# Attention into a mixer MLP: the first batch's loads cut at head three, and three batches' k pooled on GpSimd instead of TensorE

## The chip, the core and the metric

The kernel runs on one core of a Trainium2 chip. The core has five engines that run at the same time and meet only through semaphores: TensorE (PE) for matrix products, VectorE (DVE) and ScalarE (ACT) for element-wise work, GpSimd (POOL) for element-wise work and for issuing the loads that cast float32 to bf16, and SyncE (SP), which here only issues DMAs: the outputs and the transposing copies. All data moves over 16 DMA engines that the queues share. The metric is the time of one execution in microseconds of the device; smaller is better.

## What is computed

There are 8 batches, 8 heads, 576 rows and 64 columns per head. Keys and values are averaged over groups of 8 rows, so attention runs against 72 pooled rows; the result goes through a mixer (a token MLP over the rows and a channel MLP over the 512 columns), each with a residual.

```python
k_p = k.reshape(B, H, 72, 8, D).mean(axis=3)
v_p = v.reshape(B, H, 72, 8, D).mean(axis=3)
attn = softmax(scale * q @ k_p.T)              # 576 x 72 per head
x = (attn @ v_p) as (B, 576, 512)
u = x + (relu(x.T @ w_tok1) @ w_tok2).T        # 576 -> 256 -> 576
out = u + relu(u @ w_ch1) @ w_ch2              # 512 -> 1536 -> 512
```

## The kernel before

**Tiling.** The 576 rows of a batch are 512 "main" rows (four tiles of 128, row 4p+j in partition p of tile j) and 64 "tail" rows. The tails of two batches share one 128-row tile: the groups are [0,7], [1,2], [3,4], [5,6], the first of a pair in the lower half (slot 0), the second in the upper (slot 1). For groups [3,4] and [5,6] one `TailUnit` does the tail attention of both batches at once, and so needs the pooled keys of both.

**Pooled keys.** `pool_k(b)` (L259) is 32 matmuls of the raw main rows of k against a pooling matrix (L271) and 8 of the tail rows (L275), into two PSUM tiles; then four casts, two on ACT and two on DVE (L284, L285), put them block-diagonally into `kbd[b % 3]`. **Pooled values.** Batches 0 and 1 do the same by matmul (`pool_v`). From batch 2 on, v is loaded as 72 partitions of 8 rows (`vs`, L133 to 136), and GpSimd adds the 8 rows up, `sum_v` (L296): three adds for every two heads, four times, into `vpx[b % 3]`.

**The streams.** Each batch's main work, `c_stream(b)`, is the channel MLP: 12 pieces of four 512-column matmuls (L776), then 12 more (L791), three for each of four output chunks; the third of a chunk adds the residual on DVE (L801) and issues the chunk's output DMA on SP (L829). Every piece has the weight 864. A side stream, the attention of later batches, is woven between these pieces by `weave` (L29): a side item is taken when the share of side weight done is not above the share of main weight done. Main weight counts from `delay` (the second argument, 1728, that is two pieces) to `lead` (the third, 1728) before the end. An item of weight 0 is taken as soon as the item ahead of it is finished in this count. While c_stream(b) runs, the side stream holds `value_stream(b+1)` (start the transposing loads of batch b+2's q, `load_gated` for batch b+3's inputs, attention times values, the token MLP, `do_u`, and `pool_k` of a coming batch) and `score_stream(b+2)`: scores `do_S` (matmuls L330, then maximum and subtraction on DVE, L333 and L335), exponentials `do_E` on ACT (L343), transposes of the probabilities `do_PT` by DMA on SP (L350), for the two units a and c of 256 rows, then the tail unit t (L431, L437, L439, L446, L452).

**Order.** Inside `with tc.manual_schedule(engines=...)` (L854) each engine runs its instructions in exactly the order in which the Python code emits them, SP's DMAs included. Ahead of it, the set-up is ordered by the framework. An engine that waits holds up all that is behind it.

**Gates of the loads.** `load_gated(b)` (L750) first copies one element of a transposed-probability tile on GpSimd, so that the loads of batch b are not issued before; the loads and then the sums for v follow in GpSimd's order. At L739 it is called with b+2 for the batch b whose values are due.

**Batch 0** has a stream of its own (`first_stream`, L604): pool k, transpose q on PE in two halves of four heads, scores, pooled v, and so on.

Of the kernel before, what the change touches and what calls it, by code (L numbers as in the profile page):

```python
# [48 lines left out]
def kernel(  # L49
# [58 lines left out]
    half = [slice(0, TAIL), slice(TAIL, P)]  # L108
    main_t, tail_t = {}, {}
# [9 lines left out]
    def load(b, which=(0, 1, 2)):  # L119
# [9 lines left out]
        for i in which:  # L129
            src = (k, q, v)[i]  # L130
            if i == 2 and b > 1:
# [26 lines left out]
    load_main0(k, main_t[0][0], 0, H)  # L158
    load_tail0(k, tail_t[0][0])

# [7 lines left out]
    nc.gpsimd.memset(pool_m, 1.0 / POOL)  # L168
# [6 lines left out]
    nc.gpsimd.memset(diag, 1.0 / POOL)  # L175
# [5 lines left out]
    for s in range(2):  # L181
        nc.vector.memset(pool_t[s], 0.0)
        nc.vector.tensor_copy(out=pool_t[s][half[s], SPM:SP],
                              in_=diag[half[s], s * (SP - SPM):(s + 1) * (SP - SPM)])
    ident = singles.tile([P, P], BF16)
    make_identity(nc, ident)

    load_main0(q, main_t[0][1], 0, HP)
    load_main0(q, main_t[0][1], HP, H)
# [6 lines left out]
    NB = 3  # L196
    kbd = [singles.tile([P, H, 2, SP], BF16, name=f"kbd{i}") for i in range(NB)]
    vpx = [singles.tile([SP, H, D + 1], BF16, name=f"vpx{i}") for i in range(NB)]
    for i in range(NB):
        eng = nc.vector if i == 0 else nc.any  # L200
        eng.memset(kbd[i], 0.0)
        eng.memset(vpx[i][:, :, D], float(POOL))
# [4 lines left out]
    for g in range(2):  # L207
        x_tail[g] = singles.tile([P, DM], BF16, name=f"xt{g}")
        nc.any.memset(x_tail[g][half[1]], 0.0)
    for t in tail_t[1]:  # L210
        nc.any.memset(t[half[1]], 0.0)

    def clear_probs():
        for t in prob_m:
            nc.any.memset(t.rearrange("p e h n -> p (e h) n")[:, :, SP:P], 0.0)
        for t in prob_t:
            nc.any.memset(t, 0.0)
# [10 lines left out]
    def load_w_tok():  # L228
        for s in range(2):
            nc.any.memset(w1t[s][half[1 - s]], 0.0)  # L230
            nc.any.memset(w2t[s][:, :, half[1 - s]], 0.0)
# [3 lines left out]
        nc.gpsimd.dma_start(out=w1t[1][half[1], :], in_=moe_w_tok1[MAIN:S, :])  # L235
# [26 lines left out]
    def pool_k_sum(b):  # L262
        g, s = group_of[b], slot_of[b]
        km, kt = main_t[b][0], tail_t[b][0]
        kp_ps = [ps.tile([P, HP, SP], FP32, name="pa") for _ in range(2)]
        if b == 0:
            keep_running(kp_ps[0].rearrange("p r n -> p (r n)"), 22)
        for pr in range(HP):
            for j in range(NJ):
                for hl in range(2):  # L270
                    nc.tensor.matmul(out=kp_ps[hl][hl * D:(hl + 1) * D, pr, 0:SPM], lhsT=km[:, 2 * pr + hl, j, :],  # L271
                                     rhs=pool_m[:, 0:SPM], start=(j == 0), stop=(j == NJ - 1))
        for pr in range(HP):
            for hl in range(2):
                nc.tensor.matmul(out=kp_ps[hl][hl * D:(hl + 1) * D, pr, SPM:SP], lhsT=kt[:, 2 * pr + hl, :],  # L275
# [3 lines left out]
    def pool_k_copy(b, kp_ps):  # L279
        heads = kbd[b % NB].rearrange("p (r t) e n -> p r t e n", t=2)  # L280
        for hl in range(2):
            src = kp_ps[hl][hl * D:(hl + 1) * D]
# [613 lines left out]
```

## Time and profile before

| what | us |
|---|---|
| median of the runs (282.7, 284.07, 284.22) | 284.07 |
| the profiled execution's own time | 283.01 |
| its span in the trace | 281.1 |
| PE busy | 270.1 (96%) |
| DVE busy | 161.1 (57%) |
| ACT busy | 122.6 (44%) |
| POOL busy | 104.4 (37%) |
| granted TensorE clock | 1.0 throughout |

The profile is one execution on the chip. A busy time is the sum of an engine's instructions; "idle before" is the time for which an engine stood still just ahead of a group, with the instruction or DMA that ended the wait. PEld is the load of matmul weights, which overlaps the matmuls. SPq is SP's DMA queue. DMA share is the mean number of busy engines' time in the stretch. Times in the timeline and in the chain of waits are microseconds from the start of the span.

### The profile page before, as it was taken

To read this page: it belongs to the slowest core of one execution; us is meant where nothing else is said; L and a number is where in the kernel's file an instruction comes from. 1 tells how busy PE (TensorE), PEld (TensorE's weight loads), DVE (VectorE), ACT (ScalarE), POOL (GpSimd) and SP (SyncE) were. 2 spreads that over 40 slices of the span, in tenths; PEclk is the share of its full clock that TensorE was granted. 3 is DMA by queue.
4 is the path that set the end of the run, shared out by engine and by line. 5 is a ranking of instruction groups with operands and counts; after the bars stand their busy time and mean duration, and the time that the engine had idled before them with its cause. 6 is when DMAs were issued, how large, how long until landed. Compare 5 with 4: busy or idle time off the path is not lost.

```text
span 281.1 us, 5671 instructions
## 1 busy us (share of the span) xinstructions
PE 270.1 (96%) x2221; PEld 146.2 (52%) x2258; DVE 161.1 (57%) x368; ACT 122.6 (44%) x223; POOL 104.4 (37%) x153
## 2 busy tenths in 40 slices
PE   6799999999999999999999999999999999999995
PEld 4575565565445444475545454475444444554463
DVE  4695297597559952784469753775369542520012
ACT  8582896336515453045533552054514550037220
POOL 8666543590639958058429161830000000000000
PEclk9999999999999999999999999999999999999999
DMA  7999999999999999999996899659135901341013
GB/s 81 181 204 199 193 206 196 197 168 224 171 161 180 181 229 148 197 223 174 169 186 143 182 204 190 138 150 209 28 75 128 190 20 40 94 112 40 37 40 113
DMA packets 99963, 42.16 MB, mean 150 GB/s; under 512 B 69728, under 2 KB 95328, under 8 KB 99936
## 3 DMA queue, kind: packets, MB, share of 16 engines
q0 software_dynamic: 36016, 17.93, 49.2%
q1 hardware_dynamic: 63776, 23.74, 42.0%
q8 instruction: 18, 0.29, 0.4%
q10 hardware_dynamic: 144, 0.13, 0.1%
q14 instruction: 9, 0.07, 0.1%
HBM read 35.85 MB, written 9.44 MB: 161 GB/s over the span
## 4 chain that ended last, share of the span: by engine, by line
PE 84%; DMA 9%; POOL 4%; issue 1%; DVE 0%; ACT 0%; POOLq 0%
PE pa L791 33%; PE pa L776 30%; PE pa L513 4%; PE pa L479 4%; DMA qm<-in_q_dram 4%; DMA GT<-in_moe_w_tok_dram 3%; PE pa L394 3%; PE pa L330 3%; DMA pT<-prob_t 2%; PE pa L271 1%; PE pa L518 1%; PE pa L483 1%; PE pt L319 1%; POOL qm L152 1%; PE pt L357 1%
## 5 line engine op out<-in xcount | busy, mean ns | idle before, releaser
L791 PE MATMUL pa<-wc,GT 128*128 128x512 bf16 (+1 forms) x427 | 102.3, 373 | 0.9 <-issue 0.2
L778 ACT ACTIVATE GT<-pa 128x512 bf16<-128x512 f32 x105 | 62.3, 597 | 64.6 <-PE pa L776 59.5
L776 PE MATMUL pa<-uTm,wc 128*128 128x512 bf16 x356 | 88.6, 379 | 0.7
L776 PEld LDWEIGHTS <-wc 128*128 128x128 bf16 x564 | 44.9, 98 | 35.9 <-issue 0.3
L791 PEld LDWEIGHTS <-GT 128*128 128x128 bf16 x444 | 41.5, 98 | 40.7
L343 ACT ACTIVATE prob_m<-sh 128x432 bf16<-128x432 f32 (+1 forms) x48 | 24.5, 521 | 50.5 <-DVE sh L335 30.6
L302 POOL TENSOR_TENSOR s<-vs 72x512 f32<-72x512 bf16 x24 | 27.6, 1149 | 35.4 <-DMA vs<-in_v_dram 33.9
L801 DVE TENSOR_TENSOR o<-pa,um 128x512 f32<-128x512 f32 (+1 forms) x29 | 19.3, 669 | 25.3 <-PE pa L791 24.2
L335 DVE TENSOR_TENSOR sh<-pa,mx 128x432 f32<-128x432 f32 (+1 forms) x48 | 26.8, 558 | 5.1 <-ACT GT L778 0.5
L333 DVE TENSOR_REDUCE mx<-pa 128x6 f32<-128x432 f32 (+1 forms) x48 | 26.4, 550 | 3.4 <-PE pa L330 3.3
L399 DVE TENSOR_TENSOR xm<-pa,den 128x256 bf16<-128x256 f32 x56 | 23.8, 425 | 1.9
L398 DVE RECIPROCAL den<-pa 128x4 f32<-128x4 f32 (+1 forms) x66 | 11.7, 177 | 20.9 <-PE pa L394 20.7
L515 DVE TENSOR_TENSOR um<-pa,xm 128x512 bf16<-128x512 f32 x28 | 18.8, 688 | 8.1 <-PE pa L513 7.9
L475 DVE TENSOR_SCALAR AT<-pa 128x512 bf16<-128x512 f32 x8 | 5.5, 692 | 22.3 <-PE pa L483 20.8
L303 POOL TENSOR_TENSOR s<-s 72x256 f32<-72x256 f32 x24 | 17.4, 723 | 1.9
L394 PEld LDWEIGHTS <-pT 72*128 72x128 bf16 (+1 forms) x280 | 12.3, 100 | 9.7 <-issue 1.3
L330 PE MATMUL pa<-kbd,qT 128*128 128x144 bf16 x128 | 15.4, 226 | 0.5 <-ACT qT L321 0.5
L513 PE MATMUL pa<-AT,w2m 128*128 128x512 bf16 x56 | 15.8, 379 | 0.1
L330 PEld LDWEIGHTS <-qT 128*128 128x128 bf16 x128 | 10.6, 98 | 8.8 <-ACT qT L321 1.4
L394 PE MATMUL pa<-vpx,pT 72*128 72x65 bf16 (+1 forms) x280 | 14.1, 194 | 1.0 <-ACT pT L457 0.5
L479 PE MATMUL pa<-xm,w1m 128*128 128x512 bf16 x56 | 14.4, 379 | 0.1
L776 PE MATMUL pa<-uTt,wc 128*128 128x128 bf16 x192 | 11.9, 219 | 0.0
(126 smaller groups left out, 240.5 us busy)
## 6 DMA issues: line engine op xcount, KB each, us to landing
out_dram<-o SPq DMA_DIRECT2D x31, 256.0 KB, 2.8
km<-in_k_dram POOLq DMA_DIRECT2D x8, 512.0 KB, 8.5
vs<-in_v_dram POOLq DMA_DIRECT2D x8, 512.0 KB, 10.9
qm<-in_q_dram POOLq DMA_DIRECT2D x7, 512.0 KB, 12.2
wc<-in_moe_w_ch_dram POOLq DMA_DIRECT2D x6, 512.0 KB, 12.3
out_dram<-o SPq DMA_DIRECT2D x9, 128.0 KB, 2.5
kt<-in_k_dram POOLq DMA_DIRECT2D x8, 64.0 KB, 7.5
qm<-in_q_dram POOLq DMA_DIRECT2D x2, 256.0 KB, 5.1
```

Of the source, the lines that this page charges most:

```text
L302: nc.gpsimd.tensor_tensor(out=s4, in0=vs[:, hs, 0:4], in1=vs[:, hs, 4:8], op=add)
L330: nc.tensor.matmul(out=sc[:, (h - h0) * 2:(h - h0) * 2 + 2, :], lhsT=qTs[self.b][:, 2 * h + self.jj, :], rhs=kbd[self.b % NB][:, h], start ...
L333: nc.vector.tensor_reduce(out=mx[:, 0:n], in_=sc, axis=AX.X, op=ALU.max)
L335: nc.vector.tensor_tensor(out=sh[:, 0:n], in0=sc, in1=mx[:, 0:n, None].broadcast_to([P, n, SP]), op=ALU.subtract)
L343: nc.scalar.activation(out=self.probs[:, :, h0:h1, 0:SP].rearrange("p e h n -> p h e n"), in_=self.sh[i][:, 0:(h1 - h0) * 2].rearrange("p ...
L394: nc.tensor.matmul(out=ao[r, hh, :], lhsT=probs_of(h, r), rhs=vpx[b % NB][:, h, :], start=True, stop=True)
L399: nc.vector.tensor_tensor(out=xo[rows, hf * HP * D:(hf + 1) * HP * D].rearrange("p (h d) -> p h d", d=D), in0=ao[rows, :, 0:D], in1=den[ro ...
L479: nc.tensor.matmul(out=at_ps, lhsT=w1m[:, j, m * P:(m + 1) * P], rhs=x_main[b][:, j, :], start=(j == 0), stop=False)
L513: nc.tensor.matmul(out=u_ps, lhsT=w2m[:, m, j, :], rhs=ATs[b][:, m, :], start=(m == 0), stop=(m == 1))
L776: nc.tensor.matmul(out=g_ps[:, i, :], lhsT=wc1[:, kk, m * P:(m + 1) * P], rhs=uTs[:, kk, :], start=(kk == 0), stop=(kk == 3))
L778: nc.scalar.activation(out=GT[:, m0:m0 + per, :], in_=g_ps, func=AF.Relu)
L791: nc.tensor.matmul(out=hold["ps"], lhsT=GT[:, kk, j * P:(j + 1) * P], rhs=wc2[:, kk, cols], start=(kk == 0), stop=(kk == NM - 1 and us is ...
```

## The change

What it does, in four parts:

1. **Batch 0's loads.** k and q are loaded as heads 0 to 2 and heads 3 to 7 (`BANKS[0][1]` is 3), in the order k part 1, k tail, q part 1, k part 2, q part 2, v. Pooling, transposes of q and scores follow the same cut. GpSimd's set-up is now in the order of the code.
2. **Set-up work.** Zeros and constants move between engines: two pooling constants to DVE, `kbd[1]` and `kbd[2]` are cleared by ACT copies of `kbd[0]`, the probability tiles are cleared by GpSimd after the weight loads, one small weight load is moved behind the channel weights.
3. **k of batches 5, 6, 7** is loaded as `vs` is, summed on GpSimd into `ksum`, transposed by one DMA on SP into `ksT` (`ksum_T`), and copied by four DVE copies into `kbd` (`ksum_copy`); `pool_k` and the tail load of k are gone for them. The 1/8 of the mean goes into the scale of the exponential. For batch 6, `ksum_T` stands behind the scores of unit c, and the tail unit of [5,6] is emitted in the main stream, ahead of its last two pieces.
4. **Weave.** The delay of the first batch's side stream goes from 2592 to 3456.

The core of the diff:

```diff
+    KSUM = (5, 6, 7)
...
-            if i == 2 and b > 1:
+            if i == 2 and b > 1 or i == 0 and b in KSUM:
...
-    load_main0(k, main_t[0][0], 0, H)
+    HA = BANKS[0][1]
+    in_order = ExitStack()
+    in_order.enter_context(tc.manual_schedule(engines={mybir.EngineType.Pool}))
+    load_main0(k, main_t[0][0], 0, HA)
     load_tail0(k, tail_t[0][0])
+    load_main0(q, main_t[0][1], 0, HA)
+    load_main0(k, main_t[0][0], HA, H)
...
-    nc.gpsimd.memset(pool_m, 1.0 / POOL)
+    nc.vector.memset(pool_m, 1.0 / POOL)
...
+    load_main0(q, main_t[0][1], HA, H)
     ident = singles.tile([P, P], BF16)
     make_identity(nc, ident)
-    load_main0(q, main_t[0][1], 0, HP)
-    load_main0(q, main_t[0][1], HP, H)
...
+        if i == 0:
+            nc.vector.memset(kbd[i], 0.0)
+        else:
+            nc.scalar.activation(out=kbd[i].rearrange("p h e n -> p (h e n)"),
+                                 in_=kbd[0].rearrange("p h e n -> p (h e n)"), func=AF.Copy)
...
+    ksum = tail_t[0][0]
+    ksT = tail_t[0][2].rearrange("p h d -> p (h d)").rearrange("p (r n) -> p r n", n=P)
...
     def clear_probs():
-        for t in prob_m:
-            nc.any.memset(t.rearrange("p e h n -> p (e h) n")[:, :, SP:P], 0.0)
+        for t in prob_m[2:] + prob_m[:2]:
+            nc.gpsimd.memset(t.rearrange("p e h n -> p (e h) n")[:, :, SP:P], 0.0)
         for t in prob_t:
-            nc.any.memset(t, 0.0)
+            nc.gpsimd.memset(t.rearrange("p e h n -> p (e h) n")[:, :, SP:P], 0.0)
...
+    def ksum_T(b):
+        nc.sync.dma_start_transpose(out=ksT, in_=ksum.rearrange("p h d -> p (h d)"))
+
+    def ksum_copy(b):
+        heads = kbd[b % NB].rearrange("p (r t) e n -> p r t e n", t=2)
+        for hl in range(2):
+            src = ksT[hl * D:(hl + 1) * D, :, 0:SP]
+            nc.vector.tensor_copy(out=heads[0:D, :, hl, 0, :], in_=src)
+            nc.vector.tensor_copy(out=heads[D:P, :, hl, 1, :], in_=src)
...
+    def sums_of(vs, dst):
+        add = ALU.add
         for h0 in range(0, H, 2):
             hs = slice(h0, h0 + 2)
             s4 = sum_pool.tile([P, 2, 4, D], FP32, name="s4")[0:SP]
             nc.gpsimd.tensor_tensor(out=s4, in0=vs[:, hs, 0:4], in1=vs[:, hs, 4:8], op=add)
             nc.gpsimd.tensor_tensor(out=s4[:, :, 0:2], in0=s4[:, :, 0:2], in1=s4[:, :, 2:4], op=add)
-            nc.gpsimd.tensor_tensor(out=vpx[b % NB][:, hs, 0:D], in0=s4[:, :, 0], in1=s4[:, :, 1], op=add)
+            nc.gpsimd.tensor_tensor(out=dst[:, hs], in0=s4[:, :, 0], in1=s4[:, :, 1], op=add)
...
         for bb in pooled:
-            add(KP, pool_k, bb)
+            if bb in KSUM:
+                add(0, ksum_copy, bb)
+            else:
+                add(KP, pool_k, bb)
...
-        add(KP, pool_k, b)
-        add(0, warm, 3)
-        add(QT, a.do_qT, 0, HP)
-        add(QT, c.do_qT, 0, HP, copy=nc.vector.tensor_copy)
+        kp, HA = [], BANKS[0][1]
+        add(KP, lambda: kp.append(pool_k_sum(b, 0, HA, None, 13)))
+        add(0, lambda: pool_k_copy(b, kp[0], 0, HA))
+        add(0, warm, 2)
+        add(QT, a.do_qT, 0, HA)
+        add(QT, c.do_qT, 0, HA, copy=nc.vector.tensor_copy)
         add(SC, a.do_S, 0)
         add(SC, c.do_S, 0)
-        add(QT, a.do_qT, HP, H)
-        add(QT, c.do_qT, HP, H)
+        add(0, lambda: pool_k_sum(b, HA, H, kp[0]))
+        add(0, a.do_E, 0)
+        add(0, lambda: pool_k_copy(b, kp[0], HA, H))
+        add(0, warm, 3)
+        add(QT, a.do_qT, HA, H)
+        add(QT, c.do_qT, HA, H)
...
         add(SC, c.do_S, 0)
+        late = [bb for bb in own[1:] if bb in KSUM]
         for bb in own[1:]:
-            add(KP, pool_k, bb)
+            if bb not in KSUM:
+                add(KP, pool_k, bb)
         add(SC, c.do_S, 1)
         add(0, c.do_E, 0)
         add(SC, c.do_S, 2)
+        for bb in late:
+            add(0, ksum_T, bb)
         add(0, c.do_E, 1)
         add(0, c.do_E, 2)
         add(0, c.do_PT, 0)
+        for bb in late:
+            add(0, ksum_copy, bb)
         add(0, c.do_PT, 1)
+        if t and late:
+            return [(0, t.do_S), (0, t.do_E), (0, t.do_PT)]
         if t:
             add(2 * SC, t.do_S)
...
             units(b + 1)
+            for bb in owned(b + 1)[:1]:
+                if bb in KSUM:
+                    add(0, ksum_T, bb)
             add(0, qT_dma, b + 1)
...
+        if b in KSUM:
+            sums_of(main_t[b][0][0:SP], ksum[0:SP])
         sum_v(b)
...
-    clear_probs()
     load(1)
     load_w_ch2()
+    nc.gpsimd.dma_start(out=w1t[1][half[1], :], in_=moe_w_tok1[MAIN:S, :])
+    clear_probs()
     load(2, (1, 0))
...
             if b + 2 < B:
-                score_stream(side, b + 2)
-
-            weave(c_stream(b), side, (2592.0, 3456.0)[b] if b <= 1 else 1728.0, 3456.0 if b == B - 2 else 1728.0)
+                last = score_stream(side, b + 2)
+            at = len(main.items) - 2
+            main.items[at:at] = last
+
+            weave(main, side, (3456.0, 3456.0)[b] if b <= 1 else 1728.0, 3456.0 if b == B - 2 else 1728.0)
```

## The prediction

> **What bounds the kernel now.** First the page: engines, and their shares in 40 slices of 7 us.
>
> ```profile
> PE 270.1 (96%) x2221; PEld 146.2 (52%) x2258; DVE 161.1 (57%) x368; ACT 122.6 (44%) x223; POOL 104.4 (37%) x153
> PE   6799999999999999999999999999999999999995
> ```
>
> PE is busy throughout except in the head, so work taken from PE is worth its length, and a wait put on PE costs its length. Next the chain of waits, cut to the end of the stretch that runs batch 3's channel MLP:
>
> ```profile
> 149.80 0.81 PE pa L791 x3
> 150.61 0.63 PE pa L271 x32
> 151.23 0.10 PE pa L275 x8
> 151.34 0.97 PE pa L791 x4
> ...
> 153.36 0.12 PE pa L330 x2
> 153.48 0.86 PE pa L791 x4
> 154.34 0.25 PE pa L431 x16
> 154.60 3.56 PE pa L791 x16
> 158.16 1.73 PE pa L776 x8
> ```
>
> L271 and L275 are `pool_k(6)`, 0.73 us of PE. L330 x2 are unit c's last scores (c.S2), L431 the tail unit's scores of batches 5 and 6. There is no gap: PE is the bound here. Behind L431 four pieces are left (16 matmuls). Now DVE, SP and GpSimd in time order, around the same place:
>
> ```profile
> 147.11 0.60 DVE L333 TENSOR_REDUCE mx<-pa 128x6 f32<-128x432 f32 x1
> 148.34 0.60 DVE L333 TENSOR_REDUCE mx<-pa 128x6 f32<-128x432 f32 x1
> 153.40 0.69 DVE L801 TENSOR_TENSOR o<-pa,um 128x512 f32<-128x512 f32 x1
> 155.79 0.46 DVE L335 TENSOR_TENSOR sh<-pa,mx 128x288 f32<-128x288 f32 x1
> ```
>
> ```profile
> 151.68 3.06 SPq L350 DMA_TRANSPOSE pT<-prob_m  x2
> 154.83 0.53 SPq L829 DMA_DIRECT2D out_dram<-o  x1
> ```
>
> ```profile
> 132.78 0.19 POOL L752 COPY gate<-pT 128x1 bf16<-128x1 bf16 x1 [0.37 <-DMA pT<-prob_m]
> 145.32 1.14 POOL L302 TENSOR_TENSOR s<-vs 72x512 f32<-72x512 bf16 x1 [8.96 <-DMA vs<-in_v_dram]
> 155.03 0.46 POOL L304 TENSOR_TENSOR vpx<-s 72x128 bf16<-72x128 f32 x1
> ```
>
> A tile of three heads' scores costs DVE 1.23 us, one of two heads 0.92 (150.17 to 151.09), an output add 0.69. DVE lags: c.S2 leaves PE at 153.48 and DVE at 156.25. One set of sums on GpSimd takes 10.2 us (145.32 to 155.49). And the head:
>
> ```profile
> 2.19 5.46 PE L257 MATMUL pa<-idle 128*128 128x288 bf16 x22 [2.19 <-DVE pool_t L182]
> 13.94 1.02 PE L292 MATMUL pa<-vs,pool_m 128*72 128x512 bf16 x4 [0.94 <-DMA vs<-in_v_dram]
> ```
>
> PE waits for v at 13.94; from there ACT (pT copies, 15.4 to 21) and DVE (10.57 to 23.2) are full up to the batch's first channel matmul at 27.08.
>
> **Head: k and q in parts.** v is the sixth load instead of the fifth, behind the same bytes. DMA moves 170 to 190 GB/s from 4 us on, so v's landing shifts only by the start of the stream: the first issue takes 1.07 us for eight heads, about 0.75 for three (four heads took 0.78). Gain 0.3 to 0.4. Scores start some 2.5 us earlier, but everything after them still waits for v and then for ACT and DVE. I take -0.4; bounds 0 (GpSimd issues late; its four selects, 1 us, now stand ahead of q part 2) and -1.1 (DVE ends the scores that much earlier and all of it carries).
>
> **Set-up moves.** The ACT copies of `kbd[0]` (1152 elements; 1024 took 1.0 us) end near 5 us, before the first cast; cover: k's landing. If it went, 1 us. Clearing probabilities on GpSimd is 4 x 0.85 + 2 x 0.5 = 4.4 us (scaled from 0.54 for 512 elements, 0.23 for 128) in front of batch 2's loads; three channel-weight loads, 1.5 MB, are queued then, worth 7.5 us at 200 GB/s, and hide it; uncovered, up to 4.4 on loads not needed before 48 us. They don't hold up the exponentials: other columns. The batch-0 delay lets one more piece run ahead of a short wait for q at 31.7: 0 to -0.2. I take 0 for all.
>
> **PE loses three pool_k**: 3 x 0.75 = -2.3 (0.63 + 0.10, and 0.05 of issue). ACT and DVE lose two casts each; not the bound. The k tail loads of 5, 6, 7 go (0.7 us of issue each).
>
> **GpSimd gains 3 x 10.2 us**, and the gates behind them move. Batch 5: k is issued at 106, lands 6.2 later as it did, so sums of k 112.6 to 122.8, of v to 133.1 (before: 132.4); gate of batch 6 at 133.2 instead of 132.8. k of 6 lands 8.1 to 8.5 us after issue, 142; sums to 152.5, then v to 162.7; gate of 7 at about 163 to 166 instead of 163.6. `vpx` of 6, needed by the tail's values near 168, holds. Batch 7 has 10 us of slack: its k is summed by 185, its transpose stands at 193. Cost 0; were k of 6 over 4 us later, what follows would grow by the excess.
>
> **SP gains three transposes**, 1.2 us of issue each. The one for 5 (near 131) stands ahead of the q transposes, needed 10 us later; likewise for 7 (near 193). Both 0. The one for 6 is different.
>
> **Batch 6's pooled keys: a new wait on PE.** The side stream's weight in batch 3's stretch falls from 20490 to 4600 + 2160 + 3450 + 6360 = 16570; main is 24 x 864, less 1728 at each end, 17280. c.S2 is taken at 15510/16570 x 17280 + 1728 = 17903, after piece 21; all behind it, `ksum_T(6)` first, at 19008, after piece 22; and the tail scores stand exactly there too. (The same count puts the old tail scores after piece 20, as the trace has it.) So between `ksum_T(6)` and the tail scores PE has nothing to do, and SP can't run ahead: in front of the transpose stands the output DMA of chunk 2, whose last matmul is piece 21.
>
> Call Z the moment when PE reaches the tail scores. Backwards by pieces of 0.86: piece 21 ends at Z-1.0, chunk 0 and a's first scores by Z-6.9. DVE: add of chunk 0 to Z-6.2, then 1.23 + 1.23 + 0.92 + 0.69 + 1.23 + 1.23 + 0.69 = 7.2, so chunk 2's add ends at Z+1.05. Output DMA on SP 0.4 (0.33 to 0.53), transpose issued at Z+1.55. A 128x512 transpose lands in 2.4 to 5.6 us (`uTm`, `uTt`), 2.6 when DMA is fairly free as here: Z+4.2. Four DVE copies of 64x288: nearest row the 64x288 casts, 0.46; below, the reciprocal's 0.18; I take 0.35 each, 1.4. Tail scores at Z+5.75: PE stands for 5.7 us. Lower end, DVE without lag, 2.4 and 0.18: 3.5. Upper end, 5.6 and 0.46: 9.2. GpSimd's 152.5 is 1.5 us before Z (154.0), so SP, not GpSimd, sets it. Queued behind on DVE: two output adds; behind on SP: c's transposes, used 8 us later. Nobody else feels it.
>
> [...]
>
> **After the wait: PE's speed.** In the head 288 columns took 0.248 us each (5.46/22), 0.86 ns a column, against 0.42 (0.216 for 512) later: PE starts at half rate, for 5.4 us, though the granted clock reads 1.0. A gap of 0.94 us at 13 does not bring that back. 5.7 us lies between, so the loss is 0 to 2.7 us (half of 5.4); I take the middle, 1.4. [...]
>
> **Sum**, against the profiled execution's 283.0: -0.4 - 2.3 + 5.7 + 1.4 = 287.4. That execution is 1.1 below the median of 284.07 and within the runs (282.7 to 284.22), which spread by 0.5%, about what a measurement of this kernel can tell from no change.
>
> **Rivals.** (a) *The wait is short*, 3.5 or less, and PE keeps its rate: 283.0 - 2.7 + 3.5 = 283.8, no change. For it: DVE may lag less, since the casts of `pool_k` are gone. Against: the transpose's 2.4 and the output DMA ahead of it are firm. Chance 0.16. (b) *The wait is hidden*: 283.0 - 0.4 - 2.3 = 280.3, faster. It decides if `kbd` of 6 is complete by Z, which needs the transpose issued before Z-4; SP would have to be past chunk 2's output by then, and its add ends no earlier than Z-0.2 on an idle DVE. A net gain of 0.5% needs a wait under 1.3. What is left for it is a head worth 3 us more than I see. Chance 0.14. (c) *PE keeps its rate* through the full wait: 286.0. (d) *PE at half rate* for the whole 5.4: 288.7. (e) *GpSimd late*: if k of 6 lands 5 us later (loads of batches 1 to 3 took up to 16 us to land, a DMA share above 90%; here it was 8.1), the wait grows by 2 or more: 290. Chance 0.08.
>
> **Numbers.** Full wait 0.62, centre 287.4, its own range 285.5 to 289; 0.27 of it lie with (c), 0.35 with a loss of rate up to (d); with (e) 0.70 slower, less 0.02 for runs near the bound. Same 0.18, faster 0.14. The range leaves out (b) and the worst of (e): 282.6 to 290.
>
> **What would show it.** In the changed profile: L271 x160 rather than x256; a PE gap of 4 to 7 us ahead of L431, near 154, released by DVE's copies, with `ksT`'s transpose on SP issued just behind an output DMA; matmuls of 512 columns at 0.43 us behind the gap if PE slows; v's pooling in the head near 13.5; `sums_of` ending near 152.5. The prediction is wrong if the L431 gap is under 2 us, or if the first channel matmul (27.08) comes over 1 us earlier.

## The result: slower by 3.3%

| | before | after |
|---|---|---|
| median of the runs, us | 284.14 (282.70 to 285.26) | 292.73 (291.75 to 293.89) |
| ratio, 95% interval | | 1.0332 (1.0283 to 1.038) |
| the profiled execution's own time, us | 283.01 | 293.89 |
| its span, us | 281.1 | 292.2 |
| mean granted clock over the span | 1.0 | 0.982 |

The forecast was 287.4, range 282.6 to 290.0: the direction was right, the size was not. The median before has one run more here than in the table ahead of the prediction. The ratios, here and below, are formed from the runs in the chip's faster state alone, while the medians count every run. The two profiled spans are 11.1 us apart, the medians 8.6; the execution of the changed kernel that was profiled was the longest of its four. Lines such as L464 are those of the changed kernel from here on; L464 is what L431 was, the tail unit's scores.

**The page after**, PE's busy time, its 40 slices and the granted clock:

```profile
PE 272.8 (93%) x2131; PEld 144.8 (50%) x2131; DVE 164.1 (56%) x383; ACT 117.6 (40%) x208; POOL 136.1 (47%) x194
PE   6689999999999999999994499999999999999994
PEclk9999999999999999999999589999999999999999
```

Two slices of PE are at 4, and in the second of them the clock is at half. 90 instructions of PE are gone, and still it is busy for longer. Most of the loss has one place. **The chain of waits** through it (start, length, what; before, this was L791, L271, L431 without a gap):

```profile
158.83 3.32 DMA vt<-kt
...
162.17 0.23 DVE kbd L280
...
162.43 0.37 DVE kbd L281
...
162.81 1.21 DVE kbd L280
...
164.04 0.80 DVE kbd L281
...
164.88 0.40 PE pa L464 x13
165.27 3.53 PE pa L847 x8
168.80 2.78 PE pa L832 x8
```

`vt<-kt` is the transposing DMA of batch 6's k sums (`ksum_T`; it uses two old tail tiles). PE has reached the tail scores at 156.23 and, but for two matmuls in between, goes on at 164.88; its timeline:

```profile
156.23 0.22 PE L464 MATMUL pa<-kbd,qTt 64*64 64x72 bf16 x1
162.45 0.27 PE L464 MATMUL pa<-kbd,qTt 64*64 64x72 bf16 x2 [6.00 <-DVE kbd L280]
```

Behind that, 16 matmuls take 6.31 us instead of 3.46: eight of the same kind take 1.73 further down and in the profile before. **The windows** of two microseconds (their length, busy time of PE, PEld, DVE, ACT and POOL with their counts, then the granted clock, the DMA share and GB/s) tell why:

```profile
158.00:160.00 2.00, 0.00 (x0) 0.00 (x0) 0.00 (x0) 0.00 (x1) 1.84 (x3) 1.00 1.49 204
160.00:162.00 2.00, 0.00 (x0) 0.00 (x0) 0.00 (x0) 0.00 (x0) 1.84 (x3) 0.64 1.03 279
166.00:168.00 2.00, 2.00 (x6) 0.76 (x5) 1.15 (x3) 0.89 (x2) 0.00 (x0) 0.50 0.00 0
170.00:172.00 2.00, 2.00 (x16) 0.97 (x15) 0.22 (x2) 0.98 (x2) 1.10 (x3) 0.80 0.98 238
172.00:174.00 2.00, 2.00 (x18) 1.04 (x16) 1.13 (x5) 1.21 (x3) 2.00 (x4) 1.00 1.46 121
```

The clock falls to half at 160.57, some 4 us into the idle time, and comes back at 170.81, 5.9 us after PE goes on. **SP and GpSimd** ahead of it, first SP before the change, with the landing of that transposition, then SP and GpSimd after it:

```profile
132.17 1.74 SPq L553 DMA_TRANSPOSE qT<-qm  x1
...
DMA to landing us min/median/max: 3.8/3.8/3.8
```

```profile
133.21 1.27 SPq L274 DMA_TRANSPOSE vt<-kt  x1
134.57 3.03 SPq L587 DMA_TRANSPOSE qT<-qm  x1
...
158.20 0.53 SPq L885 DMA_DIRECT2D out_dram<-o  x1
158.83 1.22 SPq L274 DMA_TRANSPOSE vt<-kt  x1
```

```profile
134.57 1.29 POOL L137 DMA_DIRECT2D vs<-in_k_dram  x2 [0.44 <-issue]
...
154.54 0.45 POOL L333 TENSOR_TENSOR kt<-s 72x128 bf16<-72x128 f32 x1
```

The new transposing DMA for batch 5 stands ahead of that of batch 5's q, which now goes out at 134.57 instead of 132.17, in the same instant as the loads of batch 6. It landed 14.5 us later; before, 3.8. PE waited 0.66 us for it at 149.08:

```profile
DMA to landing us min/median/max: 14.5/14.5/14.5
...
149.08 0.36 PE L363 MATMUL pa<-kbd,qT 128*128 128x144 bf16 x3 [0.66 <-DMA qT<-qm]
```

SP's transposes behind it came late: the one that everything waits for was issued at 158.83, 3.8 us after GpSimd had finished the sums.

**The head** is late too. GpSimd's order, and PE's first value pooling (before: v issued at 5.89, pooling at 13.94):

```profile
3.71 0.92 POOL L154 DMA_DIRECT2D km<-in_k_dram  x1
4.72 0.26 POOL L176 TENSOR_SCALAR_AFFINE_SELECT pool_m<-pool_m 128x72 bf16<-128x72 bf16 x1
...
5.65 0.88 POOL L154 DMA_DIRECT2D qm<-in_q_dram  x1
...
7.06 0.90 POOL L154 DMA_DIRECT2D vs<-in_v_dram  x1
```

```profile
15.25 1.02 PE L318 MATMUL pa<-vs,pool_m 128*72 128x512 bf16 x4 [0.77 <-DMA vs<-in_v_dram]
```

The first channel matmul comes at 28.18 instead of 27.08, and up to batch 3's channel MLP (129.51 instead of 128.45) every stage is 1.06 us late.

The account of the two profiled executions: head +1.06; two poolings ahead of the wait and one behind it, 3 x 0.75, -2.25; wait for batch 5's transposed q +0.66; wait at the tail scores +8.65; half clock +2.85. That is +10.97, against +11.1 in the spans. The poolings enter with their length in the profile before; they were not measured after the change. The medians are 8.6 us apart, so some 2.4 us of the account belong to this pair of executions.

### The profile page after: what moved, and what is told of

Same layout as the page of the kernel before. It is cut to its first block, busy times and chain, and to the rows that moved or that the text cites. A ratio compares the mean times of both kernels' runs of the same rounds, so it can differ in the third digit from the quotient of the medians.

```text
span 292.2 us, 5495 instructions
## 1 busy us (share of the span) xinstructions
PE 272.8 (93%) x2131; PEld 144.8 (50%) x2131; DVE 164.1 (56%) x383; ACT 117.6 (40%) x208; POOL 136.1 (47%) x194
## 4 chain that ended last, share of the span: by engine, by line
PE 71%; DMA 11%; POOL 9%; DVE 4%; issue 2%; ACT 1%; POOLq 0%; DVEq 0%
PE pa L832 26%; PE pa L847 24%; PE pa L513 4%; PE pa L547 4%; POOL s L331 4%; DMA vs<-in_k_dram 3%; DMA vs<-in_v_dram 3%; PE pa L427 3%; DMA pT<-prob_m 3%; POOL s L332 2%; DMA uTm<-um 2%; PE pa L363 1%; DMA vt<-kt 1%; DVE sh L368 1%; PE pa L869 1%
## 5 line engine op out<-in xcount | busy, mean ns | idle before, releaser
L847 PE MATMUL pa<-wc,GT 128*128 128x512 bf16 (+1 forms) x444 | 105.7, 378 | 0.0
L832 PE MATMUL pa<-uTm,wc 128*128 128x512 bf16 x372 | 90.4, 382 | 0.5 <-DMA uTm<-um 0.5
L832 PEld LDWEIGHTS <-wc 128*128 128x128 bf16 x564 | 45.6, 98 | 38.1 <-issue 2.1
L331 POOL TENSOR_TENSOR s<-vs 72x512 f32<-72x512 bf16 x36 | 41.3, 1148 | 26.4 <-DMA vs<-in_k_dram 15.7
L332 POOL TENSOR_TENSOR s<-s 72x256 f32<-72x256 f32 x36 | 26.0, 721 | 2.8
L431 DVE RECIPROCAL den<-pa 128x4 f32<-128x4 f32 (+1 forms) x66 | 11.6, 176 | 23.2 <-PE pa L427 23.2
L549 DVE TENSOR_TENSOR um<-pa,xm 128x512 bf16<-128x512 f32 x28 | 18.8, 686 | 7.6 <-PE pa L547 7.5
L513 PE MATMUL pa<-xm,w1m 128*128 128x512 bf16 x56 | 14.4, 379 | 0.0
## 6 DMA issues: line engine op xcount, KB each, us to landing
km<-in_k_dram POOLq DMA_DIRECT2D x4, 512.0 KB, 12.4
```

The lines of the kernel that those rows point to most:

```text
L331: nc.gpsimd.tensor_tensor(out=s4, in0=vs[:, hs, 0:4], in1=vs[:, hs, 4:8], op=add)
L332: nc.gpsimd.tensor_tensor(out=s4[:, :, 0:2], in0=s4[:, :, 0:2], in1=s4[:, :, 2:4], op=add)
L513: nc.tensor.matmul(out=at_ps, lhsT=w1m[:, j, m * P:(m + 1) * P], rhs=x_main[b][:, j, :], start=(j == 0), stop=False)
L832: nc.tensor.matmul(out=g_ps[:, i, :], lhsT=wc1[:, kk, m * P:(m + 1) * P], rhs=uTs[:, kk, :], start=(kk == 0), stop=(kk == 3))
L847: nc.tensor.matmul(out=hold["ps"], lhsT=GT[:, kk, j * P:(j + 1) * P], rhs=wc2[:, kk, cols], start=(kk == 0), stop=(kk == NM - 1 and us is ...
```

## The experiments

Each variant stood beside the kernel before on the same chip; the ratios are to that one, with 95% intervals.

### Each part by itself

Batches 5 and 6 back on TensorE, and nobody on GpSimd; both are the changed kernel with one line altered:

```diff
-    KSUM = (5, 6, 7)
+    KSUM = (7,)          # first variant
+    KSUM = ()            # second variant: head and set-up alone
```

> The changed kernel with batches 5 and 6's k pooled on TensorE again; only batch 7 keeps the GpSimd sum and the transposing DMA. Theory (the loss lies in one place, the wait ahead of the tail scores of batches 5 and 6): the wait of 8.7 us and the half-rate matmuls behind it (2.85 us) go, the 0.66 us wait for batch 5's transposed q goes, and two poolings of 0.75 us come back: 292.7 - 8.7 - 2.85 - 0.66 + 1.5 = about 282 to the median of the changed kernel, 284 to 285 with its head still 1.06 us late and only one pooling saved against the kernel before; granted clock 1.0. Rival (the loss is spread: GpSimd's added sums and the transposing DMA slow every stage): with one batch of three left, a third of it stays, about 287.

> The changed kernel with no batch in the GpSimd sum: the parted first loads and the moved set-up work alone. Theory from the two traces: the first stage ends 1.06 us later, so 284.1 + 1.06 = about 285.2, with the first channel matmul near 28.2 and the v pooling of batch 0 starting near 15.2. Rival (my prediction's head): 0.4 us gained, about 283.7, v pooling near 13.5; then the late head of the profiled execution belongs to that execution.

Measured: 283.56 against 283.51, ratio 1.0017 (0.999 to 1.0044), clock 1.0 throughout, no wait over 0.5 us behind the head. And 284.93, ratio 1.003 (0.9989 to 1.0072). So the loss hangs on batches 5 and 6; the third of it that the rival left for one sum of three (287) did not stay. The set-up moves and the weave had no run of their own: they are in the second variant together with the head. The head's microsecond is below what the times can resolve, but the profiles agree on it: v pooling starts at 14.9 to 15.6 us in the seven profiles of kernels with the new head as the change has it, and at 13.6 to 14.3 in the seven with the old one.

The third part alone: the kernel before with its own loads and set-up, and with `KSUM = (5, 6, 7)`, the sums, transposes and the moved tail scores.

> The kernel before with the GpSimd sums and transposing DMAs of batches 5, 6 and 7 and the moved tail scores, and its own first loads and set-up work. Theory (the two parts of the change add up): 284.1 - 2.25 + 8.7 + 2.85 + 0.66 = about 294 minus what the sum counts twice; with the changed kernel at 292.7 and its head at +1.06, about 291.6. Rival (the late head shifts the loads against the transposes and makes the wait longer): wait under 7 us, at most 289.5.

Measured: 294.1, ratio 1.0359 (1.0301 to 1.0417). Neither expectation held: the theory's 291.6 lies just below the interval (291.6 over this comparison's 283.51 is 1.0285), the rival's 289.5 far below. PE's timeline (this kernel's L357 is the scores, L458 the tail scores):

```profile
153.21 0.54 PE L357 MATMUL pa<-kbd,qT 128*128 128x144 bf16 x3 [6.54 <-DMA qT<-qm]
...
165.66 0.22 PE L458 MATMUL pa<-kbd,qTt 64*64 64x72 bf16 x2 [3.35 <-DVE kbd L274]
166.41 0.29 PE L458 MATMUL pa<-kbd,qTt 64*64 64x72 bf16 x13 [0.53 <-DVE kbd L275]
```

Here the wait for batch 5's transposed q, 0.66 us in the changed kernel, is 6.54 us, and that at the tail scores is 4.3 us (162.09 to 166.41) instead of 8.65. Together they are 10.9 us instead of 9.3, and the clock falls to half in the first, for 6.83 us, and again 0.6 us behind the second, for 3.41. q's transposition was issued at 132.83, 0.59 us *behind* the loads of batch 6, and landed after 20.3 us. What the first wait takes, the second gets back in part; which of them is the long one went, in these two kernels, with half a microsecond between two queues.

### Is it the clock, and is it GpSimd?

The changed kernel with something for PE to do in the wait:

```diff
-            return [(0, t.do_S), (0, t.do_E), (0, t.do_PT)]
+            return [(0, lambda: warm(38)), (0, t.do_S), (0, t.do_E), (0, t.do_PT)]
```

> The changed kernel with 38 matmuls of 128x512 on unused data ahead of the tail scores of batches 5 and 6, in the place where TensorE waits for batch 6's kbd; by the 0.216 us that a matmul's stream takes at the granted clock of 1.0 they fill about 8.2 us. Nothing else is changed. Theory (behind the wait TensorE runs at half its rate for some microseconds because it had been idle; that is worth 2.85 us in the profiled execution): the wait for kbd ends at the same time, the granted clock stays 1.0 around 160 to 172 us, and the time falls by 2.85 us to about 289.9. Rival (the slow matmuls behind the wait are late for another reason, such as their operands or a clock that drops by itself): the eight matmuls behind the wait still take 3.5 us instead of 1.7, and the time stays at 292.7.

```profile
155.35 8.37 PE L268 MATMUL pa<-idle 128*128 128x512 bf16 x38
163.65 0.32 PE L464 MATMUL pa<-kbd,qTt 64*64 64x72 bf16 x16
163.90 1.90 PE L847 MATMUL pa<-wc,GT 128*128 128x512 bf16 x8
165.64 1.89 PE L832 MATMUL pa<-uTm,wc 128*128 128x512 bf16 x8
```

Measured: 291.41, ratio 1.0275 (1.0216 to 1.0334). The eight matmuls behind the wait take 1.90 us in this view instead of 3.60, the next eight 1.89 instead of 2.99. The record of the clock reads 1.00 there, where it read 0.50 in the changed kernel. So the matmuls were slow because PE had stood idle and its clock had fallen, and in this place they are worth the 2.8 us that they were booked at; from the end of the wait to the end of the span only 2.0 us are saved (125.4 against 127.3), as this execution waits elsewhere (0.7 us for a transposed u). By the medians the gain is 1.3 us, and it isn't certain: the theory's 289.9 and the rival's 292.7 both lie within the interval. The matmuls decide, not the times.

The changed kernel with GpSimd idle in the wait; it leaves out batch 6's pooled values:

```diff
-        sum_v(b)
+        if b != 6:
+            sum_v(b)
```

> The changed kernel without GpSimd's sums of batch 6's v: the pooled values of batch 6 are left out, so the result of batch 6 isn't the reference's. GpSimd is idle from the end of the k sums of batch 6, about 155 us, on. Theory (VectorE's four copies into batch 6's kbd take 2.6 us instead of 0.9 because GpSimd adds at the same time): each copy takes 0.22 to 0.23 us, as those of batches 5 and 7 do, the wait ends 1.7 us earlier, and the time is 291.0 or a little less (the clock comes back as late as before). Rival (the copies are slow because of their operands or the writing DMA): they take 0.4 to 1.2 us as before and the time is unchanged.

VectorE's four copies into batch 6's `kbd`, in the timeline (before, in the chain above, 0.23, 0.37, 1.21 and 0.80):

```profile
162.37 0.23 DVE L280 COPY kbd<-vt 64x288 bf16<-64x288 bf16 x1 [4.49 <-DMA vt<-kt]
...
163.11 0.23 DVE L281 COPY kbd<-vt 64x288 bf16<-64x288 bf16 x1
```

Measured: 290.95 (expected 291.0), ratio 1.0251 (1.0198 to 1.0303). By the times alone the gain isn't certain, as the interval overlaps that of the changed kernel; the profiles show the copies. They are 2.61 us in the one case and 0.92, four of 0.23, in the other. GpSimd's adds make the difference, and in the changed kernel each of the slow copies ends about 0.1 us behind a GpSimd add (copies to 164.02 and 164.84):

```profile
162.79 1.14 POOL L331 TENSOR_TENSOR s<-vs 72x512 f32<-72x512 bf16 x1
164.01 0.72 POOL L332 TENSOR_TENSOR s<-s 72x256 f32<-72x256 f32 x1
```

### Is it SP's order?

First the obvious repair: q's transposition back ahead of the k sums' one.

```diff
+            add(0, qT_dma, b + 1)
             for bb in owned(b + 1)[:1]:
                 if bb in KSUM:
                     add(0, ksum_T, bb)
-            add(0, qT_dma, b + 1)
```

> The changed kernel with the transposing DMA of batch 5's q issued ahead of that of batch 5's k sums instead of behind it. Theory (SP issues q's transposition 1.35 us later than before, at the moment at which the loads of batch 6 go out, and it then lands after 14.5 us instead of 3.8, and holds up all transposing DMAs behind it): it lands in about 4 us, the uT transpositions of batch 4 take 3 to 6 us as in the kernel before, SP is no longer late, the transposition of batch 6's k sums goes out at 155 to 156.5 instead of 158.8, and the wait ahead of the tail scores falls from 8.7 to about 5 to 6.5 us: time 289 to 290.5. Rival (only the order of the loads and GpSimd's sums sets it): the wait stays near 8.7 us, and at most the 0.66 us for q goes: 292.

Measured: 298.46, ratio 1.05 (1.0396 to 1.0604). Both theories missed, with the wrong sign. SP's queue, and DVE's timeline:

```profile
136.66 1.69 SPq L274 DMA_TRANSPOSE vt<-kt  x1
```

```profile
149.12 0.23 DVE L280 COPY kbd<-vt 64x288 bf16<-64x288 bf16 x1 [7.47 <-DMA vt<-kt]
...
151.81 2.48 DVE L549 TENSOR_TENSOR um<-pa,xm 128x512 bf16<-128x512 f32 x4
```

q now lands in 3.8 us, as before, but the k sums' transposition is issued 1.42 us behind the loads of batch 6 and takes 12.4. VectorE's copies for batch 5 wait for it, the residual adds of the token MLP (L549) are queued behind them, and PE waits 5.6 us for those at L552, 5.1 and 0.5 at the tail scores. The repair moved the collision to another transposition, with more behind it.

So both have to be ahead of the loads. The sums of batch 5 end at 123.8; their transposition can go out among the probabilities' of batch 4:

```diff
-        for bb in late:
+        for bb in [5] if b == 4 else late:
             add(0, ksum_T, bb)
...
-                if bb in KSUM:
+                if bb in KSUM and b != 4:
                     add(0, ksum_T, bb)
```

> The changed kernel with one step moved: the transposing DMA of batch 5's k sums is issued between the probabilities' transpositions of batch 4, near 128 to 130 us (the sums end at 123.8), instead of near 133. Theory (a transposing DMA that is issued beside or behind the loads of batch 6 lands 9 to 20 us later, one that is issued ahead of them in 2.5 to 4 us; which transposition is hit decides where TensorE waits): this one and that of batch 5's q both land in under 5 us, no wait of TensorE near 147 to 150 us, SP is on time, and the wait ahead of the tail scores of batches 5 and 6 is 5 to 7 us, since the k sums of batch 6 still end near 155 to 156: 288.5 to 290.5. Rival (SP's total of work, 1.25 us for each transposition, is what makes everything behind it late): only the order changes, and the time stays within 1 us of 292.7.

```profile
156.00 0.22 PE L464 MATMUL pa<-kbd,qTt 64*64 64x72 bf16 x1
161.51 0.27 PE L464 MATMUL pa<-kbd,qTt 64*64 64x72 bf16 x2 [5.29 <-DVE kbd L280]
164.06 0.40 PE L464 MATMUL pa<-kbd,qTt 64*64 64x72 bf16 x13 [2.29 <-DVE kbd L281]
```

Measured: 292.35, ratio 1.0332 (1.0303 to 1.0362). The mechanism held, the time did not: the two transpositions land in 2.5 and 3.8 us, nothing waits for q, SP issues batch 6's at 157.57, but the wait at the tail scores is 8.06 us. It is now 1.57 (SP's place behind two transpositions of probabilities and an output), 3.65 (landing to the first copy) and 2.79 (copies beside GpSimd). The rival's number was right; its reason, SP, covers 1.57 of the 8.06. What is left is the order: the tail scores stand right behind the transposition that they need, which the runs without the wait, below, bear out.

How long a transposition of batch 5's takes to land, against the start of the first load of batch 6:

| kernel | transposition | issued | landed after, us |
|---|---|---|---|
| q first | q | 1.74 us ahead | 3.8 |
| transposition of 5 early | q | 1.37 ahead | 3.8 |
| before | q | 1.10 ahead | 3.8 |
| tail scores behind the values (below) | q | 0.82 ahead | 6.3 |
| after | q | together | 14.5 |
| third part alone | q | 0.59 behind | 20.3 |
| q first | k sums | 1.42 behind | 12.4 |

The k sums are 512 columns, q is 2048; issued 0.75 us or more ahead of the loads, the k sums land in 2.4 to 2.6 us. The other profiles fit the rows for q: 1.02 to 1.10 us ahead, 3.8 to 3.9 (five profiles); 0.79 to 0.86 ahead, 5.9 to 6.3 (three more); together, 14.0 and 14.4 (two more).

### Without the wait

Tail scores in the next stretch, behind half of batch 5's attention values, with the old head and the early transposition:

```diff
         if t and late:
-            return [(0, t.do_S), (0, t.do_E), (0, t.do_PT)]
+            return []
...                                   # value_stream of batch 5
         add(AV, a.do_AV, 1)
+        if late:
+            add(2 * SC, t.do_S)
+            add(0, t.do_E)
+            add(0, t.do_PT)
+            add(0, load_gated, b + 2, lambda: t.pT[:, 0, 0:1])
```

> The kernel before with all three batches' k summed on GpSimd, the transposition of batch 5's sums early as in the run before, and the tail scores of batches 5 and 6, their exponentials and transposition moved into the next stretch, behind the first half of batch 5's attention values; the load of batch 7 waits for them. Theory (what the change costs is only that the tail scores come ahead of batch 6's kbd; where other matmuls stand ahead of them nothing waits): no wait of over 1 us, granted clock 1.0, three poolings saved, 3 x 0.75 = 2.25 us: 281.3 against 283.5. Rival (the moved tail scores or batch 7's load, now some microseconds later, open another wait): at or above 283.5.

Measured: 285.72 against 282.64, ratio 1.0101 (1.0068 to 1.0134): the rival held. PE's timeline (L421 attention values, L458 tail scores):

```profile
161.89 0.38 PE L421 MATMUL pa<-vpx,pT 72*128 72x65 bf16 x4 [2.73 <-DVE o L852]
...
165.29 0.33 PE L458 MATMUL pa<-kbd,qTt 64*64 64x72 bf16 x16
...
172.71 0.45 PE L421 MATMUL pa<-vpx,pT 72*64 72x65 bf16 x16 [1.29 <-DMA pT<-prob_t]
```

The tail scores no longer wait, but the four copies still stand on VectorE, 3.46 us from 157.63 to 161.12 beside GpSimd's adds, and what is queued behind them, an output add and the normalizations that free PE's output tiles, holds PE for 2.73 us; the tail unit is then late for its values, by 1.29.

Two more with the copies on ScalarE and issued in the next stretch, behind the first values in the first run, ahead of them in the second, with the tail scores one group of values earlier there:

```diff
-            nc.vector.tensor_copy(out=heads[0:D, :, hl, 0, :], in_=src)
-            nc.vector.tensor_copy(out=heads[D:P, :, hl, 1, :], in_=src)
+            copy = nc.scalar.copy if b == 6 else nc.vector.tensor_copy
+            copy(out=heads[0:D, :, hl, 0, :], in_=src)
+            copy(out=heads[D:P, :, hl, 1, :], in_=src)
```

> The run with the tail scores moved behind batch 5's attention values, with the four copies into batch 6's kbd moved behind the first of these values and from VectorE to ScalarE. Theory (there VectorE's four copies, 3.46 us beside GpSimd's sums instead of 0.9 us, held back the adds and normalizations behind them, and TensorE waited 2.7 us for these; with the tail scores 4 us late, it waited another 1.3 us for their transposition): ScalarE, which no run shows slowed by GpSimd, takes 0.35 to 0.45 us for each copy, both waits fall to under 0.5 us together, the granted clock is 1.0, and the three poolings' 2.25 us show: 280.5 to 281.5 with the kernel before at 282.6 to 283.5, a ratio of 0.992 to 0.995. Rival (any engine's copies out of these tiles are slow while GpSimd adds, or ScalarE's copies hold back the activations that TensorE waits for): copies of 0.8 us and more, waits of over 2 us, a ratio at or above 1.

> The run with the copies on ScalarE, with these copies ahead of batch 5's first attention values and the tail scores directly behind them, one group of values earlier. Theory (what was left there was one wait of 1.5 us for the transposition of the tail's probabilities, because the tail scores came too late for it): the tail scores come near 159.5 us, two us earlier, the wait for the transposition is gone, and the whole 2.25 us of three poolings show: 280.2 against 282.5, ratio 0.991 to 0.993. Rival (the copies, now as soon as the transposed sums land, hold ScalarE's queue while TensorE waits for its activations, or the tail scores wait for kbd): a new wait of 1 us or more near 158 to 160 us, ratio 0.996 or above.

Measured: 281.68, ratio 0.997 (0.994 to 1.0), and 281.40, ratio 0.9948 (0.9923 to 0.9972). In the first a wait of 1.46 us for the tail's transposed probabilities was left. In the second, ScalarE's view and PE's (here L422 values, L459 tail scores):

```profile
159.73 0.43 ACT L275 COPY kbd<-vt 64x288 bf16<-64x288 bf16 x1
```

```profile
161.54 0.29 PE L459 MATMUL pa<-kbd,qTt 64*64 64x72 bf16 x13 [0.27 <-ACT kbd L276]
...
169.57 0.45 PE L422 MATMUL pa<-vpx,pT 72*64 72x65 bf16 x16
```

GpSimd adds at the same time, and each copy takes 0.42 or 0.43 us in both runs. What is left of the 8.65 us is 0.27. The gain, 0.52% or 1.5 us (0.8 to 2.2), has the 2.25 us of three poolings just beyond its interval; waits of up to 0.9 us elsewhere (for transposed probabilities and u) stand in this profile.

The cheap way to a gain is to leave batch 6 alone: k summed for 5 and 7 (with the 1/8 in the copies, as 5 and 6 share one exponential), or for 7 only, on the kernel before.

```diff
+    KSUM = (5, 7)        # first; the transposition of 5 early
+    KSUM = (7,)          # second
```

> The kernel before with the k of batches 5 and 7 alone summed on GpSimd and transposed by DMA (the transposition for 5 early), batch 6's k pooled on TensorE with its two tails loaded as before, and the 1/8 of the mean in VectorE's four copies. Theory: the two batches whose kbd is needed a whole stage after their sums cost TensorE nothing, so 2 x 0.75 = 1.5 us are saved: 282.0 against 283.5. Rival (the transposition for batch 5 disturbs the others even when early): at or above 283.5, with a wait of TensorE near 140 to 156 us.

> The kernel before with the k of batch 7 alone summed on GpSimd and transposed by DMA. Theory (by the run with 5 and 6 back on TensorE, which stood at the time of before with a head that was 1 us late): one pooling of 0.75 us saved and nothing else, 282.75 against 283.5. Rival (GpSimd's sums and the transposition take as much from elsewhere as the pooling gives): 283.5.

Measured: 281.36, ratio 0.9966 (0.9933 to 0.9999), and 281.46, ratio 0.9956 (0.993 to 0.9983), both with the clock at 1.0 and no wait over 0.5 us behind the head. These two gains and that of the run ahead can't be told apart, so the times don't give the worth of a single pooling; all three kernels beat both the kernel before and the changed one.

### The head

The second part of q ahead of the selects, and then v too:

```diff
     load_main0(k, main_t[0][0], HA, H)
+    load_main0(q, main_t[0][1], HA, H)
+    load_main0(v, main_t[0][2], 0, H)     # second variant only
...
-    load_main0(q, main_t[0][1], HA, H)    # behind the selects
```

> As the run with the head alone, with the second part of q loaded directly behind the second part of k, ahead of GpSimd's four selects. Theory (the head is late because the four selects of GpSimd stand between two loads, and the data in flight run out at about 5 to 6 us): the rate of that microsecond rises from 93 to above 150 GB/s, v pooling starts near 14.2 instead of 15.25, and the time is about 1 us below the run with the head alone, near 284.2. Rival (the loads are late for another reason, the queue's order or smaller parts): v pooling stays near 15.2 and the time near 285.2.

> The run with q's second part loaded directly behind k's, and now batch 0's v issued directly behind that too, ahead of GpSimd's selects (near 5.5 us instead of 7.0; before the change 5.9). Theory (the changed head is late because GpSimd issues v 1.1 us later, the data in flight being too few meanwhile): v pooling starts near 13.9 to 14.2 us as in the kernel before, the first channel matmul comes near 27.2 us, and the span is 0.5 us shorter than with q alone moved. Rival (the pooling matmuls wait for the selects, now 0.9 us later, and the whole chain of k and q shifts with them): pooling of k starts near 7.4 us, the v pooling is then not behind a wait for data but behind the scores, near 14.7 us or later, and the first channel matmul stays at 27.7 us or later.

Measured: 283.56, ratio 1.0003 (0.9971 to 1.0034), and 284.28, ratio 1.0049 (1.0023 to 1.0074). PE in the first, then in the second:

```profile
6.19 0.59 PE L295 MATMUL pa<-pool_m,km 128*64 128x64 bf16 x12 [0.70 <-POOL pool_m L179]
...
14.65 1.02 PE L318 MATMUL pa<-vs,pool_m 128*72 128x512 bf16 x4 [0.36 <-DMA vs<-in_v_dram]
```

```profile
7.09 0.41 PE L295 MATMUL pa<-pool_m,km 128*64 128x64 bf16 x12 [1.60 <-POOL pool_m L180]
...
14.87 1.03 PE L318 MATMUL pa<-vs,pool_m 128*72 128x512 bf16 x4
```

The first theory was half right. v pooling comes at 14.65, so part of the microsecond was the late q; but the rate between 5 and 6 us did not rise (77 GB/s, and 73 in the second variant; 93 in the changed kernel, 195 before), so the selects don't make that hole. In the second the rival held: v no longer waits for data, the pooling of k waits 1.6 us for its constants, and all behind it shifts: the first channel matmul comes at 28.39 (27.66 in the first). GpSimd's queue is the head's limit: an issue for 3 or 5 heads takes 0.75 to 0.93 us, one for all 8 takes 0.91 (v) to 1.07 (k, the first of all), so parting k alone puts 0.78 us more in front of v. What makes the hole between 5 and 6 us was not settled; the k tail's 64 KB, whose issue takes 0.73 us with little else in flight, would fit. PE also ran slow for longer in the first variant: a matmul of 432 columns took 0.57 us at 8.63 there and 0.35 at 8.13 in the changed kernel, though the record of the clock reads 1.0 (0.997 as the mean of that execution). What that costs the head was not separated.

## Why the prediction was wrong

By the terms of its sum, against the profiled executions:

| step | predicted, us | measured, us |
|---|---|---|
| head: k and q in parts | -0.4 | +1.06 |
| set-up moves | 0 | no wait found for them |
| three poolings | -2.3 | -2.25, by their length before |
| SP's transposes for 5 and 7 | 0 | +0.66, and SP late |
| wait for batch 6's kbd | +5.7 | +8.65 |
| PE's speed behind it | +1.4 | +2.85 |
| sum | +4.4 | +10.97 |

By the medians the change is +8.6 instead of +10.97, and their 292.73 too lies beyond the range.

**Right**: the place and the kind of the loss, the pooling matmuls at x160, matmuls at 0.44 us behind the gap (3.53 over 8; forecast 0.43). The poolings' worth fits, as the account closes with it, but the variants that save one, two and three of them gain 1.2, 1.0 and 1.5 us, so it was not measured by itself. "SP, not GpSimd, sets it" held: even with the transposition of 5 out of the way, SP issued batch 6's 1.57 us after PE had reached the tail scores (forecast 1.55), while the sums had ended at 155.03, 1 us before PE was there. Ahead of it stood the output, as forecast, and two transpositions of probabilities that SP had issued until 156.85, when the output's add was done (156.78). Rival (b), a hidden wait, had the right condition (the transposition issued 4 us before PE needs it); it takes another order to meet it, as the variants without the wait show.

**Wrong, the step that failed first**: "SP gains three transposes ... The one for 5 (near 131) stands ahead of the q transposes, needed 10 us later ... 0". It was priced at SP's 1.2 us of issue. What it did was push q's transposition into the loads of batch 6, where it lands 10 us later, and keep SP busy, so that batch 6's transposition was issued 2.60 us after PE reached the tail scores instead of 1.55. That is 1.7 us (0.66 for q, 1.05 of issue) of the 6.6 by which the sum was short, and its repair alone, the run with the transposition of 5 early, left the ratio at 1.0332. The larger part is the terms that follow, each put too small: the wait in all by 2.95 (with this 1.05), the clock by 1.45, the head by 1.46.

**Wrong in size**: of the wait, issue 2.60 for 1.55, landing to the first copy 3.34 for 2.6, copies 2.67 for 1.4. The landing takes 2.5 to 2.6 us in four of the variants; what held it up here is open. Two of the copies, 0.23 and 0.37, lay within the forecast's 0.18 to 0.46, two, 1.21 and 0.80, far above: the rows that it took were of operations on PSUM, and what GpSimd's adds do to a copy from SBUF was not in the trace. In the traces the slow copies end about 0.1 us behind a GpSimd add, and undisturbed, with GpSimd idle, all four take 0.23 us; on ScalarE all eight take 0.42 to 0.43 beside the adds. No run has those on ScalarE with GpSimd idle, and why an add holds up VectorE's copy was not shown.

**The clock** was booked at half of the head's 2.7 us; 2.85 us came, since PE worked for 5.9 us, from 164.88 to 170.81, before the full rate was back. Behind six such waits in four variants it was back after 3.5 to 4.2 us of work, by our estimate a loss of 1.7 to 2.1, half of the time at half rate; in the changed kernel it came later, and why was not shown. In the traces' record of the clock the stretches at half rate in and behind these waits last 10.24 us in the changed kernel, 6.83 without v's sums and with the early transposition, 6.83 and 3.41 in the third part alone: one, two or three times 3.41. The falls in the two traces with two of them (the third part alone, q first) lie 17.07 and 17.06 us apart, five times 3.41.

**The head** failed in its sign. The forecast counted the bytes ahead of v and the shorter first issue, which took 0.93 us instead of 0.75; what decides is when GpSimd issues v, 7.06 instead of 5.89, and q's second part behind four selects. The stream moved 152 GB/s in the microsecond from 4 us before the change and 180 to 195 only from 5 us on, not 170 to 190 from 4. The late issue and the selects were named there, but only as the reason for a bound of 0.

**GpSimd's sums** were booked as ending at 152.5 and ended at 155.0: the gate opened at 133.95, 0.75 late, as batch 5's k was summed from 113.61, 8.9 us after its issue and not 6.2, and batch 6's k was summed from 144.85, 10.3 us after its issue, not 8.1 to 8.5. In the changed kernel this cost nothing, as SP was later still.

## What to carry to other kernels

Work taken off the bounding engine is worth its length only if its substitute is ready when the engine gets there: put the consumer behind other work, not right behind the last link of the chain that feeds it. A step that costs a DMA queue only its issue time must still be checked for what it pushes into a large load (here q's transposition, which then landed after 14.5 us instead of 3.8), and for what is queued, in order, behind whoever waits for it. Copies like these, bf16 within SBUF, should not stand on VectorE while GpSimd adds if a path waits for them (up to 1.22 us each here, instead of 0.23).

## What the runs showed of the hardware

- A transposing DMA of SP's (q, 2048 columns) that goes out 1.0 us or more ahead of a batch's loads on GpSimd's queue (1.6 MB) lands in 3.8 to 3.9 us, 0.8 us ahead of them in 5.9 to 6.3, together with them or 0.6 us behind in 14.0 to 20.3. Its issue on SP itself took 8.12 us instead of 1.7 in the last case. One of 512 columns 1.4 us behind took 12.4 instead of 2.5.
- A 64x288 bf16 copy from SBUF on VectorE takes 0.23 us with GpSimd idle and up to 1.22 beside GpSimd's adds; on ScalarE 0.43 beside the same adds.
- TensorE's granted clock halved in waits of 2.7 to 8.7 us, or within 0.6 us behind them, and came back after 3.41, 6.83 or 10.24 us, one, two or three times 3.41. Once it halved 2.3 us after the end of a wait of only 1.6 us, in the head with v issued ahead of the selects; waits of 1.17 us in the changed kernel's head and of 1.40 us in that of the run with q first left it at 1.0.
